# Constants made among the work, normalisation transfers on ScalarE's DMA ring, rows ordered by place then head, four output buffers

## The chip, the cores and the metric

The kernel runs on one core of one Trainium2 chip. Times are device microseconds (us) of whole executions, given as the median of several runs. A few executions of any kernel here are 1.5% or more above its fastest run; they are marked slow and are left out wherever two kernels are compared. TensorE is the matmul engine, VectorE and ScalarE the two elementwise engines that also empty PSUM, POOL is GpSimd, SP the engine that issues most DMA transfers. A ring is the DMA queue of one issuing engine.

## The reference, cut to what matters

Two attention layers over the same shape (sequence 2048, width 640, 32 heads of 20) are computed one beside the other; the outputs are joined along the last axis.

```python
# softmax half (A)
q, k, v = split(x @ wqkv)
p = softmax(einsum("bhqd,bhkd->bhqk", q, k) * Dh ** -0.5)
a = merge_heads(einsum("bhqk,bhkd->bhqd", p, v)) @ wo
# linear half (B)
phi = lambda t: where(t > 0, t + 1, exp(t)) + 1e-6
kv  = einsum("bhsd,bhse->bhde", phi(k), v)
den = einsum("bhqd,bhd->bhq", phi(q), phi(k).sum(over s)) + 1e-6
b = merge_heads(einsum("bhqd,bhde->bhqe", phi(q), kv) / den) @ wo
out = concatenate([a, b], axis=-1)
```

## The kernel before

The softmax half never forms the 2048x2048 scores. It writes q to DRAM row by row, reads rows back in shifted orders, multiplies them on VectorE into second-order products (`f_big`), and multiplies these on TensorE with tables built once from k and v (`f_Tu`, `f_TuS`). A guard checks that the norms of q and k allow this expansion. The linear half is a chain of projections, the feature map phi, one small state, and a division. Both halves then need a *normalisation*: denominators are gathered, inverted, spread to all rows of a head through DRAM, and multiplied in.

Every piece of work is a task with an assumed duration, a priority (`_C`) and dependencies. A list scheduler written in Python lays the tasks out in assumed time **while the program is built**, and this fixes the order of each engine's instructions. On the chip each engine then runs its list strictly in order, waiting on semaphores. The helper for transfers that depend on data knew one ring only:

```python
def spd(self, fns, deps, reads, writes, prio=2.0, lat=None):
    def fn(t):
        self.sch.dma_group("sp", fns, reads=reads, writes=writes)
    return self.plan.add(_Task("sp", 0.62 * len(fns), fn, prio=prio, lat=lat), deps)
```

The start emitted all constants at once, before any transpose of x:

```python
self.consts(); self.loads(); self.mid_consts()      # masks, selection matrices P, P3, M6, M2 ...
for tc in range(2):
    self.ex_[tc] = self.t_xt(tc)                    # transposes of x on TensorE, emptied by ScalarE and VectorE
```

The normalisation of three q tiles of the softmax half, and the output stage:

```python
def t_norm(self, G, evs):
    # ... gather the denominators of 6 heads x 1536 queries into 96 rows
    d1 = self.spd([... dma_start(Rc, self.OTr[120:126, r:r + 3, :] ...)], evs, ...)
    a  = self.dve(0.85, rc, (d1,))                              # reciprocal
    d2 = self.spd([... dma_start(nd ..., Rc)], (a,), ...)       # to DRAM
    nb = bass.AP(nd.tensor, nd.offset, [[1536, 6], [0, 20], [1, 1536]])     # head, then place
    d3 = self.spd([... dma_start(self.Rbc[rb][0:120] ..., nb)], (d2, ...), ...)   # broadcast, 720 KB
    m  = self.dve(1.8, mult, (d3, ...))
    self.ost[G] = self.spd(fns, (m,), ...)                      # normalised rows to DRAM (f_Od)

def t_out(self, qc, deps):
    ol = self.spd([... self.OTp[:, k] <- self.Od ...], deps, ...)   # reload of the normalised tile (f_w<-f_Od)
    for tl in range(4):
        t = 4 * qc + tl
        s = t % 2                                               # two staging buffers
        # two matmul groups of 5 -> PSUM -> self.stage[:, s, half] -> out

def q_store(self, c, qc, r):
    return bass.AP(t, o, [[self.S, nh], [nh * self.S, 20], [1, 512]])     # head, then place
```

## Time and profile before

| quantity (kernel before) | value |
|---|---|
| median of its 3 first runs | 383.33 us (383.3 to 385.23) |
| span of the profiled execution | 375.7 us (that run took 377.5 us) |
| TensorE busy | 307.5 us |
| TensorE idle, 0 to 40 / 40 to 117 / 117 to 275 / after 275 us | 17.7 / 2.0 / 16.2 / 32.3 us |
| mean granted TensorE clock | 0.927 |
| ScalarE waiting for output stores | 49.7 us |

TensorE is the engine with the most work, so its idle time, stretch by stretch, is what a better order can return. The lines behind the table are shown in the prediction.

### The profile page before, as it was taken

What the parts mean: (1) busy time and instruction counts of PE and PEld (TensorE: products, weight loads), DVE (VectorE), ACT (ScalarE), POOL (GpSimd) and SP (SyncE); (2) the same over time, 40 slices, a digit from 0 to 9 for tenths busy, and PEclk for the clock granted to TensorE, in tenths of its full rate; (3) what the DMA queues carried; (4) which work ended last, traced back from release to release, by engine and by line L of the source; (5) the groups of instructions that cost most, each with busy time, mean ns of one, the idle gap of its engine ahead of it and who ended that gap; (6) DMA issues with size and microseconds to landing.
All of it is one profiled execution on the core that took longest, in us unless ns stands there. A gap on an engine that the chain in (4) does not pass through costs nothing.

```text
span 375.7 us, 14905 instructions
## 1 busy us (share of the span) xinstructions
PE 307.5 (82%) x6814; PEld 204.6 (54%) x6814; DVE 261.6 (70%) x371; ACT 166.5 (44%) x353; POOL 11.7 (3%) x43
## 2 busy tenths in 40 slices
PE   5079899999998999897899888869867995647485
PEld 3056677887665569766577444423434562534354
DVE  6149999899979871786987998976968685330200
ACT  2049788897761462435254434322313421034043
POOL 2600000000011000000000000000000000000000
PEclk9569999999997999999999999986996999899769
DMA  8997557200145444446555769377584555744522
GB/s 275 274 195 90 100 80 244 63 30 5 31 143 164 122 144 152 121 123 184 148 169 155 207 204 258 137 231 208 172 208 136 174 178 172 205 160 145 183 92 96
DMA packets 62414, 58.02 MB, mean 154 GB/s; under 512 B 20520, under 2 KB 58824, under 8 KB 62344
## 3 DMA queue, kind: packets, MB, share of 16 engines
q1 hardware_dynamic: 61032, 55.36, 52.3%
q10 hardware_dynamic: 1312, 1.64, 1.2%
q8 instruction: 55, 0.90, 1.1%
q14 instruction: 15, 0.12, 0.1%
HBM read 38.83 MB, written 13.66 MB: 140 GB/s over the span
## 4 chain that ended last, share of the span: by engine, by line
PE 51%; DMA 17%; DVE 13%; SPq 7%; issue 4%; ACT 4%; POOL 2%; POOLq 0%; DVEq 0%; ACTq 0%
PE ps L172 51%; DMA out_dram<-f_st 9%; DMA f_big<-f_Qd 7%; SPq L1892 3%; SPq L1559 3%; DVE f_big L1572 2%; DMA f_w<-f_Od 2%; DVE f_big L1331 1%; DVE f_big L1326 1%; DVE f_r L1717 1%; DVE f_Tu L1429 1%; ACT f_ex L1721 1%; POOL f_P L1213 1%; ACT f_st L1079 1%; DVE f_pk L1731 1%
## 5 line engine op out<-in xcount | busy, mean ns | idle before, releaser
L1572 DVE TENSOR_TENSOR f_big<-f_big 120x1536 bf16<-120x1536 bf16 (+2 forms) x68 | 67.6, 1002 | 7.0 <-DMA f_big<-f_Qd 5.6
L172 PE MATMUL ps<-f_big,f_Tu 120*32 120x512 bf16 (+2 forms) x960 | 59.1, 381 | 4.8 <-DVE f_big L1572 3.3
L172 PE MATMUL ps<-f_w,f_xT 128*32 128x320 bf16 x1280 | 48.1, 306 | 11.7 <-DVE f_xT L1083 11.7
L1079 ACT CAST f_st<-ps 128x320 bf16<-128x320 f32 x64 | 25.9, 430 | 65.1 <-DMA out_dram<-f_st 49.7
L172 PE MATMUL ps<-f_wB,f_xB 128*32 128x320 bf16 x1280 | 51.0, 299 | 3.8 <-issue 3.8
L1717 DVE TENSOR_SCALAR f_r<-ps 128x320 f32<-128x320 f32 (+1 forms) x52 | 28.9, 562 | 27.7 <-ACT f_ex L1721 26.5
L172 PEld LDWEIGHTS ps<-f_w,f_xT 128*32 128x32 bf16 x1280 | 35.1, 99 | 21.5 <-DVE f_xT L1083 12.0
L172 PEld LDWEIGHTS ps<-f_big,f_Tu 120*32 120x32 bf16 (+1 forms) x960 | 31.8, 96 | 26.5 <-DVE f_big L1572 6.4
L172 PEld LDWEIGHTS ps<-f_wB,f_xB 128*32 128x32 bf16 x1280 | 38.5, 96 | 12.3 <-issue 4.8
L1079 ACT COPY f_xT<-ps 126x512 f32<-126x512 f32 (+1 forms) x29 | 16.9, 586 | 58.4 <-PE ps L172 52.3
L1721 ACT ACTIVATE f_ex<-ps 128x320 f32<-128x320 f32 (+1 forms) x52 | 26.0, 499 | 33.8 <-PE ps L172 28.7
L172 PE MATMUL ps<-f_wo,f_w 128*32 128x320 bf16 x640 | 29.6, 319 | 10.0 <-DMA f_w<-f_Od 4.7
L172 PE MATMUL ps<-f_woB,f_pk 128*32 128x320 bf16 x640 | 29.7, 330 | 3.9 <-ACT f_st L1079 3.8
L1913 DVE TENSOR_TENSOR f_pk<-ps,f_wB 128x512 bf16<-128x512 f32 x20 | 13.5, 684 | 25.4 <-DMA f_wB<-f_Bd 13.5
L1326 DVE TENSOR_TENSOR f_big<-f_big,f_Ks 128x3200 bf16<-128x3200 bf16 x16 | 29.2, 1822 | 2.2 <-ACT f_Ks L1079 2.0
L172 PE MATMUL ps<-f_xB,f_wB 128*32 128x512 bf16 x400 | 30.6, 402 | 0.0
L1331 DVE TENSOR_TENSOR f_big<-f_big 128x3200 bf16<-128x3200 bf16 x16 | 29.0, 1814 | 0.0
L172 PEld LDWEIGHTS ps<-f_wo,f_w 128*32 128x32 bf16 x640 | 19.5, 102 | 17.4 <-DMA f_w<-f_Od 8.8
L172 PE MATMUL ps<-f_xT,f_w 128*32 128x512 bf16 (+2 forms) x440 | 28.5, 403 | 0.5 <-issue 0.5
L172 PEld LDWEIGHTS ps<-f_woB,f_pk 128*32 128x32 bf16 x640 | 21.7, 106 | 10.6 <-ACT f_st L1079 5.4
L1079 ACT CAST f_big<-ps 128x320 bf16<-128x320 f32 (+1 forms) x34 | 14.8, 436 | 22.1 <-PE ps L172 21.8
L1079 ACT COPY f_Ks<-f_big 128x608 bf16<-128x608 bf16 (+1 forms) x32 | 19.1, 596 | 1.0
(113 smaller groups left out, 333.0 us busy)
## 6 DMA issues: line engine op xcount, KB each, us to landing
f_big<-f_Qd SPq DMA_DIRECT2D x20, 480.0 KB, 5.1
out_dram<-f_st SPq DMA_DIRECT2D x32, 160.0 KB, 5.5
f_Qd<-f_OTw SPq DMA_DIRECT2D x40, 120.0 KB
f_big<-f_Qd SPq DMA_DIRECT2D x20, 240.0 KB, 7.3
f_w<-f_Nd SPq DMA_DIRECT2D x4, 720.0 KB
f_Rbc<-f_Nd SPq DMA_DIRECT2D x4, 720.0 KB
f_wB<-f_Bd SPq DMA_DIRECT2D x12, 240.0 KB
f_w<-f_Od SPq DMA_DIRECT2D x4, 640.0 KB
```

The source lines that it names most:

```text
L172: lambda e: e.matmul(out, lhsT, rhs, start=start, stop=stop, tile_position=tp, skip_group_check=sgc),
L1079: return self.sch.op("act", lambda e: e.copy(out, in_), reads=reads, writes=writes)
L1213: sch.op("pool", lambda e, x=x, a=a, n=n, b=b: e.tensor_copy(self.P[:, x, 6 * a:6 * (a + n)].rearrange("p (a h) -> p a h", h=6), self.iden ...
L1326: sch.op("dve", lambda e: e.tensor_tensor(F[:, :, 122:222].rearrange("p h (d a) -> p h d a", a=20), k0.unsqueeze(2).broadcast_to([128, 32, ...
L1331: sch.op("dve", lambda e: e.tensor_tensor(F[:, :, 22:122].rearrange("p h (d a) -> p h d a", a=20), k0.unsqueeze(2).broadcast_to([128, 32, ...
L1429: sch.op("dve", lambda e: e.tensor_tensor(self.Tu[0:m, x, 0:4, :], ps[0:m, j.bank, 0:504].rearrange("p (b w) -> p b w", b=4), self.M6[0:m] ...
L1559: fns.append(lambda e, x=x, d=d, st=st, nj=nj: e.dma_start(self.slot[0:40 * nj, s, x, :], self.q_load(5, qc, d, nj, st, False)))
L1572: return e.tensor_tensor(x[:, o:o + n, :], x[:, a:a + 1, :].broadcast_to([p, n, 512]), x[:, b:b + n, :], op=ALU.mult)
L1717: sch.op("dve", lambda e: e.tensor_scalar(r1, ps[:, j.bank, 0:n], 0.0, 1e-6, op0=ALU.max, op1=ALU.add), reads=(("ps", j.bank),), writes=(( ...
L1721: sch.op("act", lambda e: e.activation(ex, ps[:, j.bank, 0:n], AF.Exp), reads=(("ps", j.bank),), writes=(("ex", k, h),))
L1892: fns.append(lambda e, k=k, p=p, q=p + n * m, src=src: e.dma_start(self.Rb[p:q, k, :], src))
L1913: sch.op("dve", lambda e: e.tensor_tensor(oT[:, c, :], ps[:, j.bank, :], self.Rb[:, k, :], op=ALU.mult), reads=(("ps", j.bank), ("Rb", k)) ...
```

## The change

Its intent: let the first projection start as soon as x is there; take the transfers of the normalisations (24 of 36 or 64 KB, and the 8 broadcasts of 720 KB) off the one crowded ring; let the broadcasts use more DMA engines; give the output stage more buffers.

```diff
 # 1. constants become tasks of low priority, after the transposes of x
-        self.mid_consts()
         for tc in range(2):
             self.ex_[tc] = self.t_xt(tc)
+        cdone = self.cdone = self.mid_consts()
+        def task(eng, dur, *ops):
+            nonlocal last
+            ...
+            last = plan.add(_Task(eng, dur, fn, prio=2.4), (last,))
+        task("dve", 1.5, ...); task("pool", 9.0, *ops); ...   # ops: 30-odd small copies on POOL
 # 2. transfers of both normalisations on ScalarE's ring, the softmax half's broadcasts too
-    def spd(self, fns, deps, reads, writes, prio=2.0, lat=None):
+    def spd(self, fns, deps, reads, writes, prio=2.0, lat=None, q="sp"):
-            self.sch.dma_group("sp", fns, reads=reads, writes=writes)
+            self.sch.dma_group(q, fns, reads=reads, writes=writes)
-        ... (("Rc", k),), prio=0.5)
+        ... (("Rc", k),), prio=0.5, q="act", lat=4.0)         # likewise four more calls
 # 3. rows by place, then head
-        nb = bass.AP(nd.tensor, nd.offset, [[1536, 6], [0, 20], [1, 1536]])
+        nb = bass.AP(nd.tensor, nd.offset, [[0, 20], [1536, 6], [1, 1536]])
-        return bass.AP(t, o, [[self.S, nh], [nh * self.S, 20], [1, 512]])
+        return bass.AP(t, o, [[self.S, 20 * nh], [1, 512]])
+        def perm(_):                                          # columns of the q weight, six copies
+            for c in range(N_DC):
+                sch.op("pool", lambda e, c=c: e.tensor_copy(
+                    self.w[:, 0, c, 0:600].rearrange("p (b a h) -> p b a h", b=5, h=6),
+                    self.w0r[:, c, 0:600].rearrange("p (b h a) -> p b a h", b=5, h=6)), ...)
+        self.ew[0] = plan.add(_Task("pool", 6.0, perm, prio=0.5), (e0,))
 # 4. four staging buffers in each half
-            s = t % 2
+            s = t % 4
-                sg = 2 + t % 2
+                sg = 4 + t % 4
 # 5. arithmetic: +1e-6 of phi(q) added at the end as a column; squares in a buffer of
 #    their own (f_Dq), guard matmuls in threes; one selection matmul in place of two;
 #    relu of phi(q) on either engine          (cut)
 # 6. the priorities _C of all task kinds set anew   (cut)
```

## The prediction

> **What bounds the kernel now.** I began with the page: busy times, then the strip of slices.
>
> ```profile
> PE 307.5 (82%) x6814; PEld 204.6 (54%) x6814; DVE 261.6 (70%) x371; ACT 166.5 (44%) x353; POOL 11.7 (3%) x43
> ...
> PE   5079899999998999897899888869867995647485
> ...
> DVE  6149999899979871786987998976968685330200
> ```
>
> TensorE is busy for 307.5 of 375.7 us, so 68.2 us of its idle time is the most that better ordering alone can return. The strip shows where that lies: a hole in the first two slices (9.4 us each), nearly none in slices 3 to 13, and ragged work from slice 26 on. The busy times by stretch size it (the first number is the length, then PE, PEld, DVE, ACT, POOL, the granted clock, the DMA share, GB/s):
>
> ```profile
> 0.00:21.00 21.00, 5.56 (x28) 2.94 (x28) 8.91 (x42) 3.24 (x5) 8.95 (x40) 0.68 0.92 270
> 21.00:40.00 19.00, 16.77 (x424) 12.11 (x428) 14.88 (x16) 15.02 (x33) 0.00 (x0) 0.90 0.82 127
> 40.00:63.00 23.00, 22.90 (x673) 17.51 (x665) 22.09 (x19) 19.25 (x43) 0.00 (x0) 1.00 0.66 144
> ...
> 304.00:340.00 36.00, 23.15 (x498) 16.19 (x494) 15.69 (x21) 8.55 (x22) 0.00 (x0) 0.95 0.57 179
> 340.00:376.00 36.00, 22.88 (x492) 15.14 (x484) 3.46 (x5) 10.11 (x24) 0.00 (x0) 0.86 0.38 126
> ```
>
> Idle of TensorE: 15.4 us before 21, 2.2 to 40, 2.0 from 40 to 117, 16.2 from 117 to 275 (158 us less 141.8 of those rows of the same view), 6.6 from 275 to 304, 26.0 after 304. So there are three regimes: a start that waits, a long middle in which TensorE and VectorE are both near full, and a tail that waits.
>
> The timeline names the waiter of the start:
>
> ```profile
> 9.47 0.59 ACT L1079 COPY f_xT<-ps 128x512 bf16<-128x512 bf16 x1 [0.27 <-PE ps L1252]
> ...
> 20.42 0.32 DVE L1239 SCALAR_TENSOR_TENSOR f_woB<-f_Rbc,f_r 128x147 bf16<-128x147 int32 x1
> 20.65 0.75 DVE L1083 COPY f_xT<-ps 128x512 bf16<-128x512 bf16 x2
> ...
> 21.12 8.81 PE L172 MATMUL ps<-f_w,f_xT 128*32 128x320 bf16 x200 [11.69 <-DVE f_xT L1083]
> ```
>
> ScalarE had evicted its three transposes of x by 10.1 us. The other two stand behind every constant in VectorE's program, and those ping-pong with POOL, so the first projection starts at 21.12.
>
> For the tail I read the waits and the chain:
>
> ```profile
> ACT f_st L1079 <- DMA out_dram<-f_st: 49.7, 8, 14.6
> ...
> PE ps L172 <- ACT f_st L1079: 14.3, 7, 6.0
> ```
>
> ```profile
> 318.30 1.07 SPq L1650
> ...
> 320.52 7.93 DMA out_dram<-f_st
> ...
> 350.59 7.14 DMA f_w<-f_Od
> ```
>
> The output stage has two buffers for each half of the output; their stores land late (median 5.5 us, up to 9.3), and ScalarE, which empties PSUM in order, holds TensorE up behind them. The last normalisation, followed by its tile, also crawls through the one DMA queue: sums gathered at 304.4, reciprocal at 311.4, its store issued only at 317.7, the broadcast at 328.0, the multiplication at 336.3, the store at 340.3, the reload at 350.6 (behind thirteen transfers for the linear half, issued from 341.2 on), and the last projection at 357.8. From the gather to that projection is 53 us.
>
> **What the Trainium skill says.** "DMA: Bandwidth & Descriptors", section "Why a DMA increments its semaphore by 16 and not by 1", says that a transfer runs on the largest number of engines, up to 16, that divides the slowest dimension of both its sides. The broadcast of reciprocals has source outer size 6 and 120 partitions, so 6 engines. The trace agrees: of its packet records of 6,144 bytes (these broadcasts alone) six are under way at once for 30.2 of the 55.3 us in which any is, and never more than seven. The same page, "Issuing engines are not separate DMA queues", says that a second issuing engine saves issue time, usually a small part of a transfer. Here issue is not small: 0.5 to 0.8 us for each of the 44 transfers that broadcast the linear half's denominators, and program order on one queue turned into 6 to 10 us steps. "TensorE: Matmul & The Clock Gate", Part 1, says that idle windows halve the clock; the granted clock is 0.68 in the first 21 us, 1.00 in full stretches and 0.86 in the last 36, so fewer holes also cheapen some matmuls. "ScalarE: Activation LUTs", its rules, would put relu on VectorE; from PSUM in fp32 the trace differs: a 128x512 ScalarE activation takes 598 ns, the VectorE relu 681 ns.
>
> **The change part by part.**
>
> *Constants among the work.* All of the constants (7 us of VectorE instructions between 3.9 and 20.7, the POOL copies from 7.8 to 15.3) become low-priority tasks after the transposes of x. The first ten transposes can be emptied by two engines as soon as x lands; it landed by 7.4 us with all of x and two weights under way, and now the first half of x and one weight go first. I put the first projection at 9.5 us: 11.6 us earlier. But the 7 us of VectorE work returns where VectorE is 86.8 of 96 us busy (21 to 117), and later slabs still come by transposing DMAs at their old times (issued to 54 us). I charge 3 us for that: net **-8.5 us**.
>
> *Rows by place then head.* The stores of q go from outer size 6 to 120 contiguous rows, 6 to 15 engines; the small ones from 2 to 10; the broadcast from 6 to 10 (20 and 120). Its 960 packets of 234 ns are 225 us of engine time, 37.5 us on each of six engines, 22.5 on ten. That frees 15 us on the first six engines, in front of which the stores of 16 engines wait. The price: POOL permutes one weight (six copies, idle engine), VectorE reads PSUM with a stride in the twelve 682 ns expansions (I assume the same time), wo takes a detour through DRAM long before its use, and the broadcasts of the linear half keep their old shape. From 117 to 275 I take 4 us of the 16.2 us of idle for this: **-4 us**.
>
> *Small transfers on ScalarE's ring.* 24 transfers of the softmax half and 8 of the linear half move: about 32 x 0.6 = 19 us of issue off SP, onto ScalarE, which has 149 us idle after 155 us. The last normalisation then needs, as an estimate from the trace's durations: gather 4, reciprocal 0.7, store 4, broadcast 6.5, multiply 1.8, store 5, reload 5.5 = 27.5 us in place of 53. The 25 us can't all be had: TensorE's own work after 304 is 46 us, and the tail holds 26 us of idle in all.
>
> *Four staging buffers for two, in each half.* The 49.7 us of ScalarE waits, of which 14.3 us reach TensorE directly, should mostly go. Together with the preceding part I take the idle after 275 from 32.6 to 15 us: **-17 us**, since a load, five matmul groups, an eviction and a store must still come last.
>
> *Arithmetic.* The +1e-6 leaves the relu for a column added at the end (some 50 one-column matmuls, about 2 us of TensorE; the same count of VectorE instructions), so 20 relus of 0.68 us may go to ScalarE, up to 13.6 us off VectorE. Squares go to a buffer of their own, three guard matmuls at a time: fewer early releases, about neutral. Selection by one matmul in place of two saves about 4 us (11 x 204 ns and 11 x 191 ns among them), where VectorE's expansion sets the pace. Sum: **-1 us**.
>
> Total: 8.5 + 4 + 17 + 1 = 30.5 us. The runs before stand at 383.3, so 353.
>
> **The rivals.** (1) ScalarE as an issuer blocks. A transfer put in its program waits there for VectorE's reciprocal or multiplication, and PSUM evictions behind it wait too, which is what stores did to SP. For it: one broadcast issue waits for store, reciprocal and an earlier multiplication, and the order is planned from assumed latencies of 4 to 6.5 us, while the landings of today scatter up to 9.3. Against: ScalarE is lightly used then. If it bites once a group (8 x 2 us), the result is 368. (2) VectorE becomes the bound in the first 117 us: 86.8 + 7 us of work in a stretch shortened to 105 is 89%; against it, VectorE idled there only 9 us. The start would then yield 4 us: 358. (3) The first six DMA engines bound the second half anyway: broadcasts of the linear half (20 x some 240 KB), the triple-row loads and a share of all else stay there. The mean share of 0.54 to 0.66 from 155 to 304 hides that imbalance. The tail would yield 8 us in place of 17: 362. (4) All the queues loosen together and TensorE runs at full clock to the end: idle of 20 us in all makes 336.
>
> **Range and chances.** The floor is TensorE's 307.5 us plus 7.6 us between this span and the unprofiled time: 315. A half of the idle time recovered is 349, a quarter 366. The start is nearly sure, the tail likely in direction but not in size. Hence 338 to 368, with 0.92 for faster by over 2% (below 375.7), 0.06 within, 0.02 slower.
>
> **What would show it right or wrong.** The first projection near 9.5 us, with VectorE's constants scattered up to 100 us; six-at-once gone from the 6,144-byte packets, ten in its place; ScalarE's wait for output stores below 15 us; gather to last reload near 28 us; TensorE idle after three quarters of the span about 15 us. It is wrong if ScalarE's queue shows long waits ahead of its transfers, if the middle gains idle time that the start gave up, or if the stores still land in 5 us or more.

## The result, and the profile after

| | before | after |
|---|---|---|
| median of 4 runs each, same rounds | 383.31 us (380.11 to 385.23) | 361.02 us (359.38 to 362.44) |
| ratio of fast runs | | 0.9425 (0.9348 to 0.9501) |
| span of the profiled execution | 375.7 us | 358.7 us |
| mean granted TensorE clock | 0.927 | 0.951 |

A ratio is the mean time of one kernel's fast runs over that of the other's of the same rounds, so it is not quite the ratio of the medians. The kernel is 5.7% faster: inside the predicted range, 8 us above the predicted value.

The page of the changed kernel, busy times and two rows of the strip (tenths of each 1/40 of the span):

```profile
PE 303.6 (85%) x6834; PEld 198.4 (55%) x6834; DVE 253.3 (71%) x350; ACT 180.1 (50%) x377; POOL 31.3 (9%) x49
...
PE   5989579999998899879988299982999868789955
...
POOL 0049880000020100000000000000000000000000
```

The hole of the first two slices is gone, and slices 34 to 38 hold 8 7 8 9 9 where they held 5 6 4 7 4. New are a dip in slices 5 and 6 ("57") and two 2s, in slices 23 and 28. POOL is now busy in slices 3 to 6, up to the end of the first dip. Busy times by stretch, same columns as the rows in the prediction (length, then PE, PEld, DVE, ACT, POOL, clock, DMA share, GB/s):

```profile
0.00:21.00 21.00, 16.86 (x284) 10.97 (x288) 9.78 (x26) 10.02 (x20) 0.86 (x7) 1.00 1.04 262
...
40.00:63.00 23.00, 16.43 (x424) 11.67 (x428) 22.29 (x19) 13.30 (x31) 12.96 (x9) 0.93 0.63 153
...
304.00:340.00 36.00, 32.26 (x814) 24.28 (x818) 12.96 (x17) 15.33 (x39) 0.00 (x0) 1.00 0.62 198
```

TensorE gained 11.3 us before 21 us (16.86 for 5.56), lost 6.5 between 40 and 63 (16.43 for 22.90), and is far fuller from 304 on (32.26 for 23.15). The timeline shows the start and the dip (start, duration, engine, line, and in brackets the idle time before and what ended it):

```profile
9.71 7.30 PE L172 MATMUL ps<-f_w,f_xT 128*32 128x320 bf16 x160
...
39.80 12.27 POOL L1157 COPY f_w<-f_Tu 128x600 bf16<-128x600 bf16 x5
...
44.08 1.81 PE L172 MATMUL ps<-f_big,f_Vp 128*32 128x242 bf16 x32 [4.38 <-DVE f_big L1362]
...
49.58 1.29 DVE L1268 TENSOR_SCALAR f_pq<-f_Rbc 128x147 f32<-128x147 int32 x1
...
52.54 1.26 PE L172 MATMUL ps<-f_xT,f_w 128*32 128x512 bf16 x20 [2.50 <-POOL f_w L1160]
```

The first projection starts at 9.71 us, as predicted (21.12 before). The dip has two parts. The second wait, 2.50 us, is for the permutation of the q weight: POOL takes 12.6 us for its six copies, from 39.80 to 52.5, where the plan assumed 6. The first wait, 4.38 us for a product of VectorE, began before the copies. VectorE had stood still until 38.93 for an index pattern that one of its own mask constants needs, and POOL made that pattern only after its selection matrices:

```profile
38.93 0.24 DVE L1268 TENSOR_SCALAR f_pq<-f_Rbc 128x147 f32<-128x147 int32 x1 [3.43 <-POOL f_Rbc L1264]
```

What the next product reads had been ready at 36.5 us, so this wait can account for up to 2.9 of the 4.38 us (an estimate from the times of the trace). Beside POOL's copies VectorE's instructions then stretch as well: the tensor_scalar of line 1268 took 0.24 us just before them and takes 1.29 beside them.

In the middle the waits of TensorE between 117 and 275 us changed their names (total us, times, longest). Before, TensorE's first two:

```profile
PE ps L172 <- DVE f_big L1572: 6.6, 7, 2.8
PE ps L172 <- issue: 6.4, 6, 2.1
```

After, TensorE's first three:

```profile
PE ps L172 <- issue: 9.2, 4, 6.7
...
PE ps L172 <- DMA f_w<-f_Od: 6.5, 1, 6.5
...
PE ps L172 <- DVE f_big L1607: 3.5, 4, 1.0
```

The products (`f_big`) hold TensorE up less. In their place stand one wait of 6.5 us for the reload of a normalised tile, and one hole of 6.66 us in which the profile shows nothing waited for. All the named waits of this stretch sum to 16.2 us before and 21.8 after, which is its idle time.

Whether transfers land sooner or later can't be read from these two traces. The medians of the view rest on the few transfers for which a landing is on record: for output stores one each of two groups after the change (3.3 and 4.2 us) and two before (1.8 and 9.3, hence the 5.5 of the prediction); for the 480 KB loads of q rows one after (8.0 us) and three before (4.8 to 5.1).

### The profile page after: what moved, and what is told of

Same layout as the page of the kernel before. It is cut to its first block, busy times and chain, and to the rows that moved or that the text cites. A ratio compares the mean times of both kernels' runs of the same rounds, so it can differ in the third digit from the quotient of the medians.

```text
span 358.7 us, 14998 instructions
## 1 busy us (share of the span) xinstructions
PE 303.6 (85%) x6834; PEld 198.4 (55%) x6834; DVE 253.3 (71%) x350; ACT 180.1 (50%) x377; POOL 31.3 (9%) x49
## 4 chain that ended last, share of the span: by engine, by line
PE 53%; DMA 15%; DVE 11%; POOL 8%; SPq 6%; issue 5%; ACT 1%; ACTq 0%; DVEq 0%
PE ps L172 52%; DMA f_big<-f_Qd 4%; SPq L1594 4%; DMA f_w<-f_Od 4%; POOL f_w L1157 3%; POOL f_st L1248 3%; DMA f_Rc<-f_xT 2%; DMA f_dc<-f_dn 2%; DMA f_pk<-in_A_x_dram 2%; DVE f_Tu L1449 2%; DMA f_wB<-f_Bd 1%; DVE f_pk L1993 1%; DVE f_big L1607 1%; DVE f_big L1357 1%; DVE f_big L1362 1%
## 5 line engine op out<-in xcount | busy, mean ns | idle before, releaser
L172 PE MATMUL ps<-f_wB,f_xB 128*32 128x320 bf16 x1280 | 52.2, 311 | 10.1 <-issue 8.0
L172 PE MATMUL ps<-f_big,f_Tu 120*32 120x512 bf16 (+2 forms) x880 | 53.4, 384 | 3.1 <-issue 1.7
L172 PEld LDWEIGHTS ps<-f_w,f_xT 128*32 128x32 bf16 x1280 | 34.3, 100 | 11.3 <-issue 0.8
L172 PEld LDWEIGHTS ps<-f_big,f_Tu 120*32 120x32 bf16 (+2 forms) x880 | 27.7, 98 | 23.2 <-issue 3.1
L1092 ACT COPY f_xT<-ps 126x512 f32<-126x512 f32 (+1 forms) x30 | 17.4, 587 | 39.2 <-PE ps L172 32.8
L172 PE MATMUL ps<-f_wo,f_w 128*32 128x320 bf16 x640 | 25.6, 320 | 6.9 <-DMA f_w<-f_Od 6.9
L1762 ACT ACTIVATE f_ex<-ps 128x320 f32<-128x320 f32 (+1 forms) x52 | 25.7, 498 | 11.3 <-PE ps L172 6.4
L1092 ACT CAST f_st<-ps 128x320 bf16<-128x320 f32 x32 | 13.3, 426 | 34.5 <-PE ps L172 30.2
L172 PE MATMUL ps<-f_woB,f_pk 128*32 128x320 bf16 x640 | 25.1, 312 | 6.4 <-DVE f_pk L1993 5.9
L1993 DVE SCALAR_TENSOR_TENSOR f_pk<-ps,f_cn,f_wB 128x512 bf16<-128x512 f32 x20 | 14.0, 745 | 21.7 <-PE ps L172 18.4
L1758 DVE TENSOR_SCALAR f_r<-ps 128x320 f32<-128x320 f32 x32 | 14.8, 485 | 18.2 <-ACT f_ex L1762 17.0
L1092 ACT CAST f_pk<-ps 128x320 bf16<-128x320 f32 x32 | 13.5, 429 | 26.1 <-PE ps L172 25.6
L172 PEld LDWEIGHTS ps<-f_wo,f_w 128*32 128x32 bf16 x640 | 19.3, 103 | 12.9 <-DMA f_w<-f_Od 7.9
L172 PEld LDWEIGHTS ps<-f_woB,f_pk 128*32 128x32 bf16 x640 | 17.8, 101 | 13.5 <-DVE f_pk L1993 7.9
L1627 ACT ACTIVATE f_Dq<-f_big 120x512 bf16<-120x512 bf16 (+1 forms) x24 | 15.1, 628 | 13.2 <-DMA f_big<-f_Qd 11.3
```

Of the source, the lines that this page charges most:

```text
L172: lambda e: e.matmul(out, lhsT, rhs, start=start, stop=stop, tile_position=tp, skip_group_check=sgc),
L1092: return self.sch.op("act", lambda e: e.copy(out, in_), reads=reads, writes=writes)
L1627: sch.op("act", lambda e: e.activation(self.Dq[0:120 if c < 5 else 40, dq, :], src, AF.Square), reads=(k0,), writes=(("Dq", dq),))
L1758: sch.op("dve", lambda e: e.tensor_scalar(r1, ps[:, j.bank, 0:n], 0.0, 1e-6, op0=ALU.max, op1=ALU.add), reads=(("ps", j.bank),), writes=(( ...
L1762: sch.op("act", lambda e: e.activation(ex, ps[:, j.bank, 0:n], AF.Exp), reads=(("ps", j.bank),), writes=(("ex", k, h),))
L1993: sch.op("dve", lambda e: e.scalar_tensor_tensor(oT[:, c, :], ps[:, j.bank, :], self.cn[:, c:c + 1], self.Rb[:, k, :], op0=ALU.add, op1=AL ...
```

## The experiments

**Theory and rivals.** The theory at this point, called A in the records below: the constants are worth some 5 us because POOL's permutation gives back the rest; four staging buffers, ScalarE's ring and the ten-engine broadcast each carry a part of the gain; and none of them is worth its part alone, since the kernel before has another wait ready. The rivals: a part does nothing (the ring saves only issue time, the engine count does not matter, new priorities alone explain the gain), or one part alone brings all of it.

Kernels marked "removed" start from the changed kernel and take one part out; kernels marked "alone" start from the kernel before and put one part in. In the removed ones, except the priorities, the plan is kept, so every engine keeps its order, and only what is executed or buffered differs. That order was tuned with all the parts in place, so what a removal costs includes the loss from an order that no longer fits; the two are not separated. All results agreed with the reference. "us" is the median; where slow runs are among them, the mean of the fast runs is given beside it.

### The changed kernel again

No edit; it shares chip and rounds with the next three.

> The changed kernel again, as the measure for the other runs. A: the 6.7 us hole of TensorE at 199.6, which the profile puts down to nothing, comes from its program (an instruction fetch held up by a burst of transfers) and is there again within 2 us of its place. Rival: it is chance, and this profile has none over 2.5 us. Time 359 to 363 us either way.

Measured: 359.84 us, three fast runs with mean 358.96 and one slow of 364.96; ratio 0.9426 (0.9348 to 0.9504), the same as the first time. The profile fell in the slow run (span 363.1). Its idle time by the four stretches is 7.5, 7.2, 26.0 and 17.9 us against 6.7, 8.3, 21.9 and 18.3; from a slow run no difference is explained. The hole of 6.66 us ends at 206.21 us, where the first trace of the changed kernel had it end at 206.26, so it came in both executions of this program:

```profile
206.26 2.06 PE L172 MATMUL ps<-f_wB,f_xB 128*32 128x320 bf16 x28 [6.66 <-issue]
```

### Removed: permutation on POOL (put on ScalarE)

```diff
-                sch.op("pool", lambda e, c=c: e.tensor_copy(
+                sch.op("act", lambda e, c=c: e.copy(          # likewise the sixth copy
```

> The permutation of the q weight on ScalarE in place of POOL, every engine's order else unchanged. A: the POOL copies (12.6 us, 39.8 to 52.5) took back the gain of the start, by the 2.5 us wait for them and by slowing VectorE, which lost some 4 us beside them: copies of 0.7 us, VectorE's feature products at 1.82 us again, idle of TensorE from 40 to 63 us down from 6.6 to 2 to 3 us, and the run 3 to 6 us faster than the changed kernel. Rival: the stretch is held by VectorE's load of constants: idle stays over 5 us and the time within 1.5 us of it. A second rival: the gain comes at 63 us and is lost again in the middle.

Measured: 361.43 us, two fast runs with mean 358.04; ratio 0.9491 (0.9371 to 0.961). No difference in time. The timeline says why:

```profile
36.85 6.39 ACT L1157 COPY f_w<-f_Tu 128x600 bf16<-128x600 bf16 x5
...
44.02 1.52 PE L172 MATMUL ps<-f_w,f_xT 128*32 128x320 bf16 x20 [6.20 <-ACT f_big L1092]
...
49.45 0.23 DVE L1268 TENSOR_SCALAR f_pq<-f_Rbc 128x147 f32<-128x147 int32 x1
```

The same five copies take 6.39 us on ScalarE, where POOL took 12.27, and VectorE's line 1268 is back at 0.23 us. So what stretched VectorE was the work on POOL. The stretching is mutual. In the run with the constants first, further below, POOL's copies of this line (number, then shortest, median and longest in ns) were:

```profile
L1157 POOL COPY f_w<-f_Tu x5: 1277/1294/2734, 28.2 to 34.4; 128x600 bf16<-128x600 bf16 x5
```

There the copies at 30.39 and 31.74 us, beside which VectorE ran no product, took 1.28 us each, as long as on ScalarE, and the one beside a product took 2.73. In the changed kernel four of the five have VectorE's products beside them and take 2.54 to 2.77. The Trainium skill, "SBUF — State Buffer", section "Who interferes with whom", says that VectorE and GpSimd share one pair of SBUF ports as an exclusive lock; the two traces agree in direction (0.24 to 1.29 us beside the copies, 0.23 without). But now TensorE waits 6.20 us for an eviction queued behind the copies on ScalarE. TensorE's idle up to 117 us is 14.8 us, against 15.0. The wait changed engines: a copy of this length in front of a busy engine's evictions costs as much as one that shares its time with VectorE. VectorE's wait for the index pattern is in this run too (3.41 us). The mechanism of the expectation was right, the gain in time was not there.

### Removed: ScalarE's ring

```diff
-            self.sch.dma_group(q, fns, reads=reads, writes=writes)
+            self.sch.dma_group("sp", fns, reads=reads, writes=writes)
```

> The 32 small transfers of the two normalisations issued by SP at the same places in the order, all else unchanged. A: ScalarE's ring is what shortened the tail: SP runs them late behind its stores and broadcasts, ScalarE loses its waits, the last gather-to-reload grows from 36 to 45 us or more, and the run is 6 to 14 us slower than the changed kernel. Rival (the reading of the Trainium skill): only issue time is saved, the time is within 2 us. Second rival: ScalarE's blocking costs more than it brings, 2 to 5 us faster.

Measured: 370.02 us, fast runs 369.08; ratio 0.9751 (0.9657 to 0.9846). The ring is worth 10.1 us (369.08 less 358.96, same chip and rounds), so the rival's 2 us falls. That the cause is more than issue time is not shown: in this trace SP spends 20.7 us on issuing these 32 transfers. From the gather of the last normalisation to the issue of its reload it is 51.4 us (279.25 to 330.66), against 36.3 (284.96 to 321.27). TensorE's idle after 275 us is 17.9 us, though, no more than with the ring; in this trace the loss lies between 117 and 275 (27.1 us of idle against 21.9) and in 2.5 us more of busy time. The kernel has more of its work left at 275 us, too (72.5 us of TensorE, against 65.4). One trace does not settle where the ring's 10 us arise.

### Removed: four staging buffers (two again)

```diff
-                    self.copy(x.eng, self.stA[s][:, hc], ...  (("st", s, h),))
+                    self.copy(x.eng, self.stA[s % 2][:, hc], ...  (("st", s % 2, h),))
                                       # the store, and the linear half's stB, likewise
```

> Two staging buffers in each half again, the order of all engines unchanged. A: the other two buffers took away ScalarE's waits for output stores (49.7 us before): those waits come back with 10 to 30 us and the run is 4 to 9 us slower than the changed kernel. Rival: stores land in 3.3 to 4.2 us now for 5.5 before, since they no longer queue behind broadcasts on six engines, and two buffers would do: within 2 us.

Measured: 377.6 us, fast runs 375.92; ratio 0.9962 (0.9861 to 1.0063). This one part is worth 17.0 us, twice what was expected: without it the rest of the change gains nothing. The waits show the old pair back, ScalarE on stores and TensorE on ScalarE:

```profile
ACT f_st L1092 <- DMA out_dram<-f_st: 25.4, 8, 7.8
...
PE ps L172 <- ACT f_st L1092: 17.3, 6, 6.7
```

TensorE's idle after 275 us is 29.9 us, with 18.3 in the changed kernel and 32.3 before. The plan of the changed kernel packs output groups close together on the assumption of four buffers, so two hurt it more than they hurt the kernel before, where 14.3 us reached TensorE.

### Removed: broadcast on ten engines (six again)

```diff
-        nb = bass.AP(nd.tensor, nd.offset, [[0, 20], [1536, 6], [1, 1536]])
+        nb = bass.AP(nd.tensor, nd.offset, [[1536, 6], [0, 20], [1, 1536]])
```

The destination rows stay in the new order, so this source belongs to other rows. It was meant as a wrong result for the sake of the timing; it stayed within the tolerance all the same.

> The changed kernel with the softmax half's broadcast read head first again (outer size 6), all else unchanged; the result is wrong on purpose in that half, the work is the same. A: ten engines for six unload the first six: six packets of 6,144 bytes at once again for most of the time, output stores and loads of products land later, 3 to 6 us slower than the changed kernel. Rival: the bytes are the same and the broadcasts overlap other work, within 2 us. Second: the 6.7 us hole of TensorE near 206 us comes from ten engines being filled at once and vanishes here, 2 to 6 us faster.

Measured first: 368.38 us, but only one of its four runs was marked fast (359.84). Its profile is that fast run: the hole of 6.66 us is gone (the longest wait called "issue" is 2.8 us), and still the middle idles 23.8 us. So the hole is not what makes the middle long: without it other waits take its place (4.7 us for the squares, 4.6 for the reload). It was run again with five rounds:

> The kernel with broadcasts on six engines once more, since three of its four runs were marked slow and the fourth as fast as the changed kernel. If the scatter of 360 to 374 us is its own, these runs scatter again and their median is 4 to 8 us over the changed kernel: ten engines pay. If it was the chip, they stand at 358 to 362 us: the number of engines does nothing to the time.

Measured: 367.85 us, four fast runs with mean 366.65; ratio 0.962 (0.955 to 0.969). The intervals do not overlap: ten engines are worth 0.0195 x 381 = 7.4 us. Six packets of 6,144 bytes are under way at once for 26.7 us here and 30.2 before; with ten engines it is ten at once for 11.4 us, and the time with any under way falls from 55 us (before) to 46.

### Removed: constants among the work (emitted first again)

```diff
             def fn(t):
-                for f, r, w in ops:
-                    sch.op(eng, f, reads=r, writes=w)
-            last = plan.add(_Task(eng, dur, fn, prio=2.4), (last,))
+            for f, r, w in ops:
+                sch.op(eng, f, reads=r, writes=w)
+            last = plan.add(_Task(eng, dur, lambda t: None, prio=2.4), (last,))
```

> The changed kernel with all its constants made before the transposes of x, as before, the order else unchanged. A: the start is worth what TensorE was ahead of the kernel before at 117 us, 4.7 us: first projection near 20 us again, run 3 to 6 us slower than the changed kernel. Rival 1: the gain of the start is lost on the way, within 1.5 us. Rival 2: it is worth its whole 11.4 us, 9 us or more slower.

Measured: 366.23 us, all four runs fast, mean 366.94; ratio 0.963 (0.9539 to 0.9722), so 0.0205 x 381 = 7.8 us slower than the changed kernel by the ratios; the two traces differ by 5.2 us (363.9 and 358.7). The old wait of the start is back in the waits:

```profile
PE ps L172 <- DVE f_xT L1096: 11.7, 1, 11.7
```

TensorE idles 18.1 us before 40 (6.7), but only 1.8 from 40 to 117 (8.3): 19.9 against 15.0 in all, 4.9 us. The idle of the middle is equal (21.2 and 21.9). So the start gains, in the traces, about half of what the first projection gains (it starts at 20.29 us here), and that half does reach the end.

### Alone: four staging buffers in the kernel before

```diff
+        self.stA = [self.stage[:, 0], self.stage[:, 1], w1[:, 5120:5760], w1[:, 5760:6400]]
+        self.stB = [self.stage[:, 2], self.stage[:, 3], ks[:, 0:640], ks[:, 640:1280]]
-                    self.copy(x.eng, self.stage[:, s, hc], ...  (("st", s, h),))
+                    self.copy(x.eng, self.stA[t % 4][:, hc], ...  (("st", t % 4, h),))
```

> The kernel before with four staging buffers in each half and nothing else, its order unchanged. A: the wait for output stores was the tail's bound by itself: ScalarE's 49.7 us of waits fall below 15 us and the run is 8 to 14 us faster than before. Rival: SP's late normalisation and broadcasts bound the tail too, and take the place of that wait: 1 to 4 us faster.

Measured: 377.63 us; ratio 0.9874 (0.9777 to 0.997). ScalarE's 49.7 us of waits for stores are gone, and 14.3 of them had reached TensorE, yet the gain is 1.3%, 4 to 5 us (377.39 against 381.11 in the means), where the same part is worth 17 in the changed kernel. Other waits of TensorE grew in their place (the profiled run, 379.62 us, is the slowest of the four):

```profile
PE ps L172 <- DVE f_pk L1916: 13.6, 4, 5.8
...
PE ps L172 <- DVE f_big L1575: 9.6, 9, 3.3
PE ps L172 <- ACT f_big L1592: 8.0, 4, 4.9
```

They were 7.5, 6.6 and 1.9 us. The first is the linear half's multiplication by its reciprocals. Idle after 275 us goes from 32.3 to 30.0 only.

### Alone: ScalarE's ring in the kernel before

```diff
-            self.sch.dma_group("sp", fns, reads=reads, writes=writes)
+            self.sch.dma_group(q, fns, reads=reads, writes=writes)    # q="act" in the five small transfers
```

> The kernel before with the 32 normalisation transfers on ScalarE's ring and nothing else, order unchanged. A: the normalisation chain is short then but stores still have two buffers, so half of the 10 us that the changed kernel loses without it: 3 to 7 us faster than before. Rival 1: as ScalarE is blocked by the stores' buffers, the transfers behind it come as late as on SP: within 2 us. Rival 2: ScalarE's blocking makes it slower.

Measured: 383.84 us; ratio 1.0065 (0.999 to 1.014): nothing, or a little slower. ScalarE still waits 48.8 us for the output stores (two buffers), and the transfers that it issues come no earlier than on SP: from the last gather to the issue of the last reload it is 48.6 us (305.2 to 353.8), against 46.2 before (304.4 to 350.6).

```profile
ACT f_st L1079 <- DMA out_dram<-f_st: 48.8, 8, 14.6
```

### Exchanged: the priorities

```diff
-_C = dict(q=1.13, qs=0.0, ... out=2.0, ... bo=0.82, ... tf=0.61, npo=2.08, ...)
+_C = dict(q=1.24, qs=0.0, ... out=0.46, ... bo=0.03, ... npo=2.33, ...)     # and the reverse
```

The changed kernel with the old priorities, planned anew:

> The changed kernel with the priorities of before in its host-side planning, so its operations in another order; the constants, rows, ring and buffers of the change stay. A: buffers and ring pay only in an order that uses them (undone in the changed kernel they cost 16 and 10 us, put alone into the kernel before they brought 3 and nothing), so the denominators of the linear half come late again and the run is 8 to 15 us slower than the changed kernel. Rival: the parts carry the gain and the numbers are fine tuning, within 3 us.

Measured: 369.01 us, only two of four runs fast (mean 364.69), so no ratio. Against 0.9425 x 381.29 = 359.4 us for the changed kernel in those rounds it is about 5 us slower; on two runs that is an indication. Its TensorE never waits for a normalised tile (the output groups come later), yet its middle idles 21.3 us and its end from 275 on 23.0. The kernel before with the new priorities, planned anew:

> The kernel before with the new priorities and nothing else. A: without the buffers and the ring the new order has nothing to use: between 3 us faster and 10 us slower than before. Rival: the order alone carries the tail's gain, 8 us or more faster than before.

Measured: 381.29 us; ratio 1.0016 (0.9953 to 1.0078). The new order is worth nothing without the buffers and rings that it was tuned for.

### Added: POOL permutes first, with its true duration in the plan

In the changed kernel POOL makes selection matrices until 38.7 us, for a first use at 112.4 us, then two index patterns, and permutes only then. Here the plan gets the measured durations, and those matrices wait for the permutation.

```diff
-        self.ew[0] = plan.add(_Task("pool", 6.0, perm, prio=0.5), (e0,))
+        self.ew[0] = plan.add(_Task("pool", 12.6, perm, prio=0.5), (e0,))
-        task("pool", 9.0, *ops)
+        task("pool", 15.0, *ops, after=self.ew[0])
```

> The changed kernel with POOL's copies for the selection matrices made to wait for the permutation of the q weight, both with the durations that the trace showed, and the order planned anew. A: the q projections start near 44 us instead of 52.5, idle of TensorE from 40 to 63 us falls from 6.6 to 3 us or less and the run is 2 to 5 us faster than the changed kernel. Rival: the gain at 63 us is given back in the middle, as with the permutation on ScalarE: within 1.5 us. Second rival: the new order is worse by chance, 3 us or more slower.

Measured: 358.38 us, four fast runs with mean 357.4; ratio 0.9385 (0.9318 to 0.9451). The permutation starts as soon as its weight has landed, at 28.7 us, 11 us earlier than in the changed kernel:

```profile
28.72 11.63 POOL L1157 COPY f_w<-f_Tu 128x600 bf16<-128x600 bf16 x5 [27.45 <-DMA f_Tu<-in_A_wqkv_dram]
...
52.08 1.25 PE L172 MATMUL ps<-f_xT,f_w 128*32 128x512 bf16 x20
```

TensorE's idle from 40 to 117 us falls from 8.3 to 4.7, and the q projection at 52.08 waits for nothing. Two things changed at once: with the masks behind the permutation, VectorE's wait of 3.43 us for the index pattern is gone too, so this run does not say how much each is worth. It has the lowest mean of all the kernels, but its interval overlaps that of the changed kernel (0.9348 to 0.9501): a gain of about 0.4% is likely and not shown.

### All runs in one table

| kernel | us | fast mean | ratio to before | idle 0-117 / 117-275 / end |
|---|---|---|---|---|
| before | 383.31 | | 1 | 19.7 / 16.2 / 32.3 |
| changed | 361.02 | 360.97 | 0.9425 | 15.0 / 21.9 / 18.3 |
| changed, again (slow profile) | 359.84 | 358.96 | 0.9426 | 14.7 / 26.0 / 17.9 |
| permutation on ScalarE | 361.43 | 358.04 | 0.9491 | 14.8 / 22.4 / 17.0 |
| without the ring | 370.02 | 369.08 | 0.9751 | 14.3 / 27.1 / 17.9 |
| without four buffers | 377.60 | 375.92 | 0.9962 | 15.1 / 22.5 / 29.9 |
| without ten engines (5 rounds) | 367.85 | 366.65 | 0.962 | 14.3 / 25.6 / 21.9 |
| constants first | 366.23 | 366.94 | 0.963 | 19.9 / 21.2 / 20.6 |
| old priorities | 369.01 | 364.69 | none | 12.9 / 21.3 / 23.0 |
| POOL permutes first | 358.38 | 357.40 | 0.9385 | 12.3 / 24.2 / 17.4 |
| before + four buffers | 377.63 | 377.39 | 0.9874 | 19.6 / 17.9 / 30.0 |
| before + ring | 383.84 | 383.72 | 1.0065 | 19.7 / 18.6 / 35.3 |
| before + new priorities | 381.29 | 381.40 | 1.0016 | 18.8 / 19.7 / 30.6 |

Removed one at a time, the five parts cost 10.1 (ring), 17.0 (buffers), 7.4 (engines), 7.8 (constants) and about 5.3 us (priorities): 47.6 us, over twice the 22.3 us of the whole change. Added one at a time, the three that could be added bring +0.7%, -1.3% and +0.2%. They do not add. That each takes away a wait behind which the next already stands is the reading that fits; no run with two parts alone tests it.

## Why the prediction was right or wrong

The rows of the two traces (before, then changed) for the stretches from 40 us on:

```profile
40.00:117.00 77.00, 75.02 (x1992) 55.54 (x1984) 71.94 (x76) 58.72 (x128) 1.83 (x2) 1.00 0.37 95
117.00:275.00 158.00, 141.77 (x2989) 89.62 (x2992) 126.68 (x189) 62.39 (x125) 0.95 (x1) 0.95 0.58 169
275.00:375.70 100.70, 68.41 (x1400) 44.36 (x1388) 39.16 (x53) 27.14 (x63) 0.00 (x0) 0.90 0.50 159
...
40.00:117.00 77.00, 68.73 (x1744) 47.80 (x1744) 73.11 (x74) 55.15 (x120) 14.80 (x11) 0.98 0.46 120
117.00:275.00 158.00, 136.13 (x2970) 86.96 (x2970) 118.78 (x173) 65.06 (x132) 0.95 (x1) 0.92 0.66 173
275.00:358.70 83.70, 65.42 (x1361) 40.10 (x1356) 37.02 (x53) 35.20 (x75) 0.00 (x0) 0.95 0.54 170
```

The sum of the prediction against them (TensorE's idle by stretch, and its busy time):

| term | predicted | measured |
|---|---|---|
| start, up to 117 us | -8.5 | 19.7 to 15.0: -4.7 |
| middle, 117 to 275 | -4 | 16.2 to 21.9: **+5.7** |
| end, after 275 | -17 | 32.3 to 18.3: -14.0 |
| arithmetic (busy time) | -1 | 307.5 to 303.6: -3.9 |
| sum | -30.5 | -16.9 (span: -17.0) |

At 275 us TensorE has done 239.1 us of work in the trace before and 238.2 in the changed one, so the whole lead of 17.0 us arises after that. The -3.9 is not arithmetic alone: kernels with the changed arithmetic have busy times from 301.3 us (permutation on ScalarE) to 307.5 (old priorities).

**The start: mechanism right, size half.** The step "I put the first projection at 9.5 us" held to 0.2 us. The step that was mis-sized is "I charge 3 us for that": the return was 6.3 us (idle from 40 to 117 went from 2.0 to 8.3). It was charged to VectorE's load, and the prediction called POOL, which got the six copies, an "idle engine". POOL was making selection matrices until 38.7 us, VectorE stood 3.43 us behind them, and the copies took 12.6 us where 6 were planned, because VectorE's products ran beside them. The run with POOL permuting first returns 3.6 us of idle; the run on ScalarE shows that no engine was free enough to take the copies for nothing. Rival 2, which made the start yield 4 us, had the size. VectorE's own constants did hold TensorE up, but by a wait for POOL and not by their 7 us of work.

**The middle: the step failed, with its sign.** "From 117 to 275 I take 4 us of the 16.2 us of idle for this" came out as 5.7 us more. The DMA part of it was right as a mechanism: ten packets at once, and 7.4 us lost without them. But the idle did not fall. Transfers are not the only thing in this stretch: TensorE's waits for products fell by 3.1 us, and a wait for a reload (+6.5) and "issue" holes (+2.8) took more than their place. No single wait is the cause: the kernel without the big hole idles 23.8 us there, the one without the reload wait 21.3. All the kernels that carry the change's data layout and arithmetic idle 21.2 to 27.1 us in this stretch, all those without it 16.2 to 19.7, from one trace each. Which piece does it (the guard matmuls in threes on a buffer of their own and the relus on ScalarE are candidates) was not told apart and stays open. The prediction named "if the middle gains idle time that the start gave up" as a sign of being wrong, and it came: the start gave up 4.7 us, the middle gained 5.7. Yet it is not the start's lead handed back: with the constants first the middle idles as long (21.2 us).

**The end: right, and nearly in size.** ScalarE's store waits are gone from the list (49.7 us before; below 15 predicted), and idle after 275 is 18.3 us, not 15. TensorE's longest wait there, 3.43 us up to 293.76, is for a product that stands behind the reciprocal in VectorE's order, and VectorE itself waits 3.33 us there for the gather. The last normalisation was predicted at 27.5 us from gather to projection; it took 42.7 us (284.96 to 327.7), in place of 53. The gather landed after 7.4 us instead of 4, the broadcast was issued 6 us after the store instead of 4 and was multiplied in 9.2 us later instead of 6.5, and SP's own order put 10.4 us between the store and the reload (310.9 to 321.3), where 5 were taken. Here the "estimate from the trace's durations" took good cases for typical ones. That it cost only 3 us fits what the prediction itself named as the cap: TensorE had other work meanwhile. What it had wrong is the weight of the two parts: it credited ring and buffers together, and in the traces the idle of the end depends on the buffers (29.9 us without them) and not on the ring (17.9 without it).

**The conversion: wrong, and luck for the total.** The floor used "7.6 us between this span and the unprofiled time". A run is only 1.8 us longer than its span in every run listed (377.5 and 375.7; 360.54 and 358.7). The other 5.8 us were the profiled run of the kernel before being faster than its fellows. Of the 22.3 us between the medians the two traces therefore show 17.0; the missing 5.3 are in slower executions of the kernel before that no trace shows. That the time came within 8 us of 353 is luck to that extent: in the traces the sum missed by 13.6.

**The rivals.** (1), ScalarE blocking as an issuer, is seen, and with it the prediction's sign of "long waits ahead of its transfers". Before eight of its 32 transfers ScalarE stands still, after its previous instruction, for 0.8 to 3.5 us, 14.2 us in all, with PSUM evictions or relus behind; the profile names some of these waits after another engine:

```profile
293.19 0.32 ACTq L1690 DMA_DIRECT2D f_Nd<-f_Rc  x1
293.56 0.60 ACT L1767 ACTIVATE f_r<-ps 128x512 f32<-128x512 f32 x1 [3.84 <-DVE f_Rc L1688]
...
307.92 0.58 ACTq L1953 DMA_DIRECT2D f_Bd<-f_dc  x1
308.54 1.48 ACT L1092 CAST f_st<-ps 128x320 bf16<-128x320 f32 x4 [4.07 <-DVE f_xB L1781]
```

It costs less than the ring brings, since the kernel without the ring has none of these waits and is 10.1 us slower. Of (3), that the first six engines bound the second half, it is shown that taking six again for the broadcasts costs 7.4 us; its size for the tail, 8 us, was not met (14.0). (4) falls.

Three readings in the prediction need correcting. The transfers that broadcast the linear half's denominators are 52, not 44. The 234 ns of a broadcast packet is the median; all 960 sum to 265.5 us, not 225. The median landing of 5.5 us stands on two stores.

In the traces the sum missed mainly by the middle (9.7 us), then by the start (3.8) and the end (3.0), less 2.9 of busy time. That the parts' gains can be sized separately and summed was a further assumption, which none of the rivals questions: the buffers gave 4 to 5 us alone and 17 in company, the ring none alone and 10 in company.

## What to carry to other kernels

Where several waits stand one behind the other, a part of a change has no worth of its own: test it by taking it out of the finished kernel as well as by adding it to the old one, and expect the two to differ. Moving work to an idle engine is free only if it is idle at the moment when the input lands; look at what stands before it in that engine's program, and measure the duration there, beside what runs at the same time, before a scheduler plans with it. And compare a profiled run with its own run time before using the difference from a median as overhead.

## What the Trainium skill lacked or had wrong

- "DMA: Bandwidth & Descriptors", "Issuing engines are not separate DMA queues", calls the saving of a second issuing engine usually small. In the changed kernel 32 transfers put back on one ring cost 10.1 us of 359, while in the kernel before the second ring brought nothing (ratio 1.0065). The section does not say that a transfer also stands behind the waits of those before it in its issuer's program: in the kernel before, the last reciprocal began at 311.4 us, took 0.74, and its store was issued at 317.7. How much of the 10.1 us is this and how much issue time is not separated.
- "SBUF — State Buffer", "Who interferes with whom", has the shared port, but not the size for strided bf16 copies on POOL: a 128x147 tensor_scalar of VectorE went from 0.24 to 1.29 us, 128x3200 products from 1.82 to between 2.13 and 2.88, and POOL's own copies from 1.28 to 2.77.
- No page looked at gives the cost of a strided 128x600 bf16 copy: 1.28 us on POOL without VectorE's products beside it, 2.54 to 2.77 with them, 1.28 on ScalarE (6.39 / 5).
- "Runtime: NRT & Kernel Launch", "Instruction fetch mechanics", says that the cost of crossing a block of 16 KiB of instructions is mostly hidden. In the changed kernel TensorE stood for 6.66 us in the middle of a group, waiting for nothing that the profile shows, at the same place in two runs. The 16,384-byte instruction packets were 13.3 us apart there, the longest distance of this trace; others of 9 to 12.6 us stand where no such hole is. That a late fetch was the cause is not shown.
- "ScalarE: Activation LUTs", "Rules for kernel authors", sends relu to VectorE, with a reason that it gives for bf16. For fp32 from PSUM the rule does not hold here: 0.60 us on ScalarE (128x512, line 1767 of the changed kernel), and in the kernel before 0.68 on VectorE.
